# The x transposes of a gated mix of linear attention and a token MLP: from TensorE to DMA, with the first loads in another order

## The chip, the cores and the metric

The kernel runs on one core of a Trainium2 chip. The metric is the device time of one execution in microseconds; the median of three runs of the kernel before is 162.86 us (162.6 to 163.35). Lower is better.

## The reference

The input `x` has 2048 tokens of 512 features, in bfloat16. Two branches work on it and a gate mixes them.

```python
g = sigmoid((x * gate_w).sum(-1, keepdims=True))
# branch A: linear attention, 32 heads of 16
q, k, v = heads(x @ wqkv)
phi = lambda t: where(t > 0, t + 1, exp(t)) + 1e-6
kv = einsum("bhsd,bhse->bhde", phi(k), v);  z = phi(k).sum over s
o = einsum(phi(q), kv) / (einsum(phi(q), z) + 1e-6);  a = o @ wo
# branch B: an MLP over the tokens, after a layer norm over the features
h = layernorm(x);  u = gelu(einsum("bsd,sf->bdf", h, w1) + b1)
b = (einsum("bdf,fs->bds", u, w2) + b2) transposed back
out = g * a + (1 - g) * b
```

`wqkv` is 512 x 1536, `wo` 512 x 512, `w1` 2048 x 1792 and `w2` 1792 x 2048.

## The kernel before, in words

Tokens are cut into 16 tiles of 128 (`NT`), features into four blocks of 128 (`ND`). Two layouts of x are kept on the chip: `xs`, with tokens on the partitions, which is a plain load, and `xT`, with features on the partitions. TensorE multiplies over the partitions, so the projections to q and k need `xT`; the layer norm, the gate and the products below need `xs`.

The scheduler is off (`tc.manual_schedule()`, L123): each engine and each queue runs its instructions in the order of the program, and PSUM is a ring of eight banks, all of one tag. DMAs that SP and ACT issue share eight completion semaphores in turn, so the ninth DMA is issued only when the first has landed, and so on.

The stages of TensorE are, in order:

1. `warm_up`: matmuls on a constant, while the first loads are under way.
2. A head for tiles 0 to 2 (`HEADS = 3`): twelve 128x128 transposes on TensorE against an identity (`transpose_part`, through the helper on L110), whose results DVE (L212) and ACT (L210) copy from PSUM to `xT` (`copy_part`); the k projection of these tiles is put between them in parts (`k_part`), and the layer-norm statistics of tiles 0 and 1 (`ln_step`) follow on DVE.
3. The K loop, tiles 3 to 15: four matmuls of the k projection (`kacc <- wk_sb, xT`), then `k_phi`, which is an exponential on ACT (L216) and two instructions on DVE (L217, L220) that give `pk`; then, four tiles behind (`LAG = 4`), four matmuls that add x^T phi(k) of one tile into four banks that stay held (`g_tile`, `gacc <- pk, xs`); then, five tiles behind, the layer-norm statistics of one tile on DVE (L240, L241).
4. The last four `g_tile`, and then the first third of the MLP's first product (`uacc`) with the q projection (`qacc`) put between, the rest of `uacc`, and per token tile the output of branch A (`aps`) and the second product of the MLP (`yps`).

The head and the K loop hold 64 `kacc` and 64 `gacc` matmuls of 512 columns in all.

The loads go out on two queues. SP issues x tile 0, x tile 1, block 2 of Wk; then, after a small copy on DVE (L156) that writes two columns of `xT` and needs x tile 0, the DMA transposes of tiles 3 to 4 and 5 to 7 straight from memory into `xT` (`load_xT`, L132), then x tiles 3 and 4 to 7, then the transposes of 8 to 11, x 8 to 11, the transposes of 12 to 15, x 12 to 15, Wq, and the MLP's first weights in chunks. ACT issues blocks 0 and 1 of Wk, x tile 2 and block 3 of Wk.

Of the kernel before, what the change touches and what calls it, by code (L numbers as in the profile page):

```python
# [7 lines left out]
ACT = mybir.ActivationFunctionType  # L8
# [7 lines left out]
def kernel(  # L16
# [13 lines left out]
    nc = tc.nc  # L30
    P = nc.NUM_PARTITIONS
# [9 lines left out]
    ND = D // P  # L41
# [24 lines left out]
    def keep(shape, dtype, name):  # L66
        return persist.tile(shape, dtype, name=name, tag=name)

    def bank(name, dtype=FP32):
        return ps.tile([P, SC], dtype, name=name, tag="bank")  # L70

    xs = keep([P, NT, D], BF16, "xs")
    hs = keep([P, NT, D], BF16, "hs")
    xT = keep([P, ND, S], BF16, "xT")
# [15 lines left out]
    ident = keep([P, P], BF16, "ident")  # L90
# [18 lines left out]
    def mm(o, lhsT, rhs, start, stop, **kw):  # L109
        nc.tensor.matmul(o, lhsT=lhsT, rhs=rhs, start=start, stop=stop, **kw)  # L110
# [14 lines left out]
    def load_x(q, t0, n):  # L125
        q.dma_start(out=xs[:, t0 : t0 + n, :], in_=x_view[:, t0 : t0 + n, :])

    def load_wk(q, k, n):
        q.dma_start(out=wk_sb[:, k : k + n, :], in_=wqkv_view[:, k : k + n, D : 2 * D])

    def load_xT(t0, n):
        nc.sync.dma_start(  # L132
            out=xT[:, :, t0 * P : (t0 + n) * P], in_=X[t0 * P : (t0 + n) * P, :], transpose=True
        )

    load_x(nc.sync, 0, 1)
    load_wk(nc.scalar, 0, 2)
    load_x(nc.sync, 1, 1)
    load_x(nc.scalar, 2, 1)
    load_wk(nc.sync, 2, 1)  # L140
    load_wk(nc.scalar, 3, 1)
    nc.vector.memset(ones_f[:], 1.0)
    nc.vector.memset(mhalf[:], -0.5)
    nc.gpsimd.memset(ident[:], 0.0)
# [1 line left out]
        out=ident[:], in_=ident[:], compare_op=ALU.not_equal, fill=1.0, base=0,  # L146
# [5 lines left out]
        out=maskQ[:], in_=maskH[:].rearrange("p (a m) -> p m a", m=2), op=ALU.max, axis=AX.X  # L152
    )
    nc.gpsimd.memset(brow[:], 0.0)

    nc.vector.tensor_copy(  # L156
        out=xT[:, :, 3 * P : 3 * P + 2],
        in_=xs[:, 0, 0 : 2 * ND].rearrange("p (k c) -> p k c", k=ND),
    )
    load_xT(3, 2)  # L160
    load_xT(5, 3)
    load_x(nc.sync, 3, 1)
    load_x(nc.sync, 4, 4)
    for t0, n in ((8, 4), (12, 4)):
        load_xT(t0, n)
        load_x(nc.sync, t0, n)
    nc.sync.dma_start(out=wq_sb[:], in_=wqkv_view[:, :, 0:D])
    w1c = []
    for c, (j0, nb) in enumerate(w1_chunks):
        w = wpool.tile([P, NT, FB * P], BF16, name="w1c", tag="wc")  # L170
        w1c.append(w)
        for t0 in range(0, NT, 8) if c == 0 else (0,):
            t1 = t0 + 8 if c == 0 else NT
            nc.sync.dma_start(
                out=w[:, t0:t1, : nb * P], in_=w1_view[:, t0:t1, j0 * P : (j0 + nb) * P]
# [6 lines left out]
    def load_small():  # L182
        nc.gpsimd.dma_start(out=brow[0:NF, :], in_=B_b1.rearrange("(f q) -> f q", q=P))
        nc.gpsimd.dma_start(out=brow[NF : NF + NT, :], in_=B_b2.rearrange("(f q) -> f q", q=P))
        nc.gpsimd.dma_start(
            out=gw_b[:], in_=gate_w.rearrange("(o d) -> o d", o=1).to_broadcast([P, D])
        )
# [3 lines left out]
    def warm_up(n, cols=SC):  # L191
        for _ in range(n):
            mm(wps[:, :cols], warm[:, 0:P], warm[:, :cols], True, True)

    act_warm = keep([P, 1], FP32, "act_warm")
    nc.scalar.activation(out=act_warm[:], in_=ones_f[:], func=ACT.Exp)
    warm_up(6)

    pts = {}

    def transpose_part(t, k0, k1):
        pt = pts[t, k0, k1] = bank("pt")
        for k in range(k0, k1):
            mm(pt[:, k * P : (k + 1) * P], xs[:, t, k * P : (k + 1) * P], ident[:], True, True)

    def copy_part(t, k0, k1, on_act):
        src = pts.pop((t, k0, k1))[:, k0 * P : k1 * P].rearrange("p (k s) -> p k s", k=k1 - k0)
        dst = xT[:, k0:k1, t * P : (t + 1) * P]
        if on_act:
            nc.scalar.activation(out=dst, in_=src, func=ACT.Copy)  # L210
        else:
            nc.vector.tensor_copy(out=dst, in_=src)  # L212

    def phi(dst, acc):
        e = work.tile([P, SC], BF16, name="e", tag="e", bufs=6)
        nc.scalar.activation(out=e[:], in_=acc[:], func=ACT.Exp)  # L216
        nc.vector.tensor_scalar(  # L217
            out=e[:], in0=e[:], scalar1=1.0, scalar2=PHI_EPS, op0=ALU.min, op1=ALU.add
        )
        nc.vector.scalar_tensor_tensor(  # L220
            out=dst, in0=acc[:], scalar=0.0, in1=e[:], op0=ALU.max, op1=ALU.add
        )
# [3 lines left out]
    def k_part(t, ks):  # L226
        if t not in kaccs:
            kaccs[t] = bank("kacc")
        for k in ks:
            mm(  # L230
                kaccs[t][:], xT[:, k, t * P : (t + 1) * P], wk_sb[:, k, :],
                k == 0, k == ND - 1,
            )

    def k_phi(t):
        phi(pk[:, t, :], kaccs.pop(t))

    def ln_stats(t):
        stats = work.tile([P, nc.vector.BN_STATS_DIM], FP32, name="stats", tag="stats", bufs=2)
        nc.vector.bn_stats(out=stats[:], in_=xs[:, t, :])  # L240
        nc.vector.bn_aggr(out=mv[:, t, :], in_=stats[:])  # L241

    def ln_rstd(g):
        s = slice(g * TPC, (g + 1) * TPC)
        nc.vector.tensor_scalar_add(out=veps[:, s], in0=mv[:, s, 1], scalar1=EPS)
        nc.gpsimd.tensor_tensor(out=rstd[:, s], in0=veps[:, s], in1=mhalf[:], op=ALU.pow)

    def ln_shift(g):
        s = slice(g * TPC, (g + 1) * TPC)
        nc.vector.scalar_tensor_tensor(  # L250
            out=nmr[:, s], in0=mv[:, s, 0], scalar=-1.0, in1=rstd[:, s],
            op0=ALU.mult, op1=ALU.mult,
        )

    def ln_apply(t):
        nc.scalar.activation(  # L256
            out=hs[:, t, :], in_=xs[:, t, :], func=ACT.Identity,
            scale=rstd[:, t : t + 1], bias=nmr[:, t : t + 1],
        )
# [3 lines left out]
    def g_tile(t):  # L263
        if not gacc:
            gacc.extend(bank("gacc") for _ in range(ND))
        for k in range(ND):
            mm(gacc[k][:], xs[:, t, k * P : (k + 1) * P], pk[:, t, :], t == 0, t == NT - 1)
# [15 lines left out]
    def ln_step(u):  # L283
        ln_stats(u)
        if u % TPC == TPC - 1:
            ln_rstd(u // TPC)

    HEADS = 3
    for k0, k1 in ((0, 1), (1, 2), (2, ND)):
        transpose_part(0, k0, k1)  # L290
        copy_part(0, k0, k1, k0 == 2)
    k_part(0, range(2))
    for k0, k1 in ((0, 1), (1, 2), (2, ND)):
        transpose_part(1, k0, k1)
    for k0, k1 in ((0, 2), (2, ND)):
        transpose_part(2, k0, k1)
    copy_part(1, 0, 1, False)
    copy_part(1, 1, 2, True)
    copy_part(2, 0, 2, False)
    copy_part(2, 2, ND, True)  # L300
    copy_part(1, 2, ND, False)
    k_part(1, range(2))
    k_part(2, range(2))
    ln_step(0)
    for t in range(HEADS):
        k_part(t, (2,))
    for t in range(HEADS):
        k_part(t, (3,))
        k_phi(t)
    ln_step(1)  # L310
    LAG = 4
    LN_LAG = 5
    APPLY = 10
    for t in range(HEADS, NT):
        k_part(t, range(ND))
        k_phi(t)
        if t >= LAG:
            g_tile(t - LAG)
        if t > LN_LAG + 1:
            ln_step(t - LN_LAG)  # L320
        if t == TPC - 1 + LN_LAG:
            load_small()
        if t >= APPLY:
            ln_apply(t - APPLY)
        if t in (TPC + LN_LAG, 2 * TPC + LN_LAG):
            ln_shift((t - LN_LAG) // TPC - 1)
# [133 lines left out]
    for j in range(NB0, NF):  # L460
        c, jj = divmod(j, FB)
# [30 lines left out]
        out=gg[:], in0=gth[:], scalar1=0.5, scalar2=0.5, op0=ALU.mult, op1=ALU.add  # L492
    )
    nc.vector.tensor_scalar(
        out=c1[:], in0=gth[:], scalar1=-0.5, scalar2=0.5, op0=ALU.mult, op1=ALU.add
# [3 lines left out]
    for t in range(NT):  # L499
        c, tl = divmod(t, TPC)  # L500
        aps = bank("aps")
        for j in range(ND):
# [3 lines left out]
            out=a_sc[:], in_=aps[:], func=ACT.Identity,  # L506
            scale=gg[:, t : t + 1], bias=c2[:, t : t + 1],
        )
        for c0, W in ((0, 2 * P), (2 * P, P), (3 * P, P)) if t == NT - 1 else ((0, D),):
            cs = slice(c0, c0 + W)  # L510
            yps = bank("yps")
            for f in range(NF):
# [6 lines left out]
                out=ot[:, :W], in0=yps[:, :W], scalar=c1[:, t : t + 1], in1=a_sc[:, cs],  # L519
# [35 lines left out]
```

## Time and profile before

| | |
|---|---|
| median of the runs | 162.86 us (162.6 to 163.35) |
| span of the profiled execution, first to last instruction | 160.8 us |
| median less span | 2.06 us |
| TensorE busy | 156.3 us, 97% of the span |
| DVE busy | 124.8 us, 78% |
| ACT busy | 72.8 us, 45% |
| start of the first MLP matmul, which ends the K stage | 32.49 us |

The profile shows one execution. The record lists no time of its own for it besides the span; the 2.06 us between span and median lie around the program. "PE" is TensorE's matmuls, "PEld" its weight loads, which overlap them. A matmul of 512 columns is listed with 379 ns, but the next one starts some 216 ns after it, since matmuls are pipelined: four take 0.86 us. "SPq" and "ACTq" are the queues on which SP and ACT issue DMAs; the time of such a row is that of issuing, and the landing of the data is listed apart.

### The profile page before, as it was taken

How to read it: one execution, taken by the hardware profiler on the slowest of the kernel's cores; microseconds unless marked ns; L12 is line 12 of the kernel's file. 1: busy time of each engine (PE TensorE's matmuls, PEld its weight loads, DVE VectorE, ACT ScalarE, POOL GpSimd, SP SyncE). 2: the span in 40 equal slices, each digit the busy share in tenths (PEclk: the TensorE clock that was granted, in tenths of full speed). 3: DMA queues.
4: the chain of work that ended last, by engine and by line, in shares of the span. 5: the costliest groups of instructions: out<-in, count | busy, mean ns of one | idle time of the engine just before them, and what ended most of it. 6: DMA issues, size and time to landing. Idle time of an engine off the chain costs nothing.

```text
span 160.8 us, 2241 instructions
## 1 busy us (share of the span) xinstructions
PE 156.3 (97%) x826; PEld 72.6 (45%) x840; DVE 124.8 (78%) x276; ACT 72.8 (45%) x114; POOL 7.3 (5%) x17
## 2 busy tenths in 40 slices
PE   7999999999999999999999999999999999999993
PEld 2444444444444444444444444444444444444462
DVE  1599999769999998756999999676999999711122
ACT  3552476654978483059873330237433442111110
POOL 3000332002020000000000000000000000000000
PEclk9999999999999999999999999999999999999999
DMA  5999999999970007600930689501000001110001
GB/s 165 229 235 238 274 335 295 359 348 348 335 177 0 0 0 236 225 0 5 335 120 2 186 270 288 169 33 37 33 33 33 33 33 60 47 60 33 33 33 33
DMA packets 29369, 22.94 MB, mean 143 GB/s; under 512 B 7824, under 2 KB 29328, under 8 KB 29360
## 3 DMA queue, kind: packets, MB, share of 16 engines
q1 hardware_dynamic: 28400, 21.89, 46.1%
q10 hardware_dynamic: 848, 0.79, 1.4%
q0 software_dynamic: 112, 0.14, 0.7%
q8 instruction: 6, 0.10, 0.3%
q14 instruction: 3, 0.02, 0.0%
HBM read 19.01 MB, written 2.10 MB: 131 GB/s over the span
## 4 chain that ended last, share of the span: by engine, by line
PE 94%; DVE 3%; issue 1%; ACT 0%
PE uacc L110 30%; PE yps L110 30%; PE aps L110 9%; PE qacc L110 8%; PE gacc L110 8%; PE kacc L110 7%; PE wps L110 2%; DVE pk L220 1%; DVE e L217 1%; DVE stats L240 0%; ACT e L216 0%; PE kvps L110 0%; PE pt L110 0%; PE w2ps L110 0%; DVE ot L518 0%
## 5 line engine op out<-in xcount | busy, mean ns | idle before, releaser
L110 PE MATMUL uacc<-hs,w1c 128*128 128x512 bf16 (+1 forms) x230 | 51.2, 379 | 0.3 <-issue 0.2
L110 PE MATMUL yps<-uT,w2c 128*128 128x512 bf16 (+2 forms) x247 | 50.8, 355 | 0.3
L110 PEld LDWEIGHTS <-w2c 128*128 128x128 bf16 x252 | 23.6, 98 | 25.2
L110 PEld LDWEIGHTS <-w1c 128*128 128x128 bf16 (+1 forms) x233 | 21.8, 98 | 26.0 <-issue 0.2
L505 ACT ACTIVATE a_sc<-aps,c,gg 128x512 f32<-128x512 f32 x16 | 12.4, 774 | 31.2 <-PE aps L110 15.5
L518 DVE SCALAR_TENSOR_TENSOR ot<-yps,c,a_sc 128x512 bf16<-128x512 f32 (+2 forms) x18 | 12.3, 688 | 15.4 <-PE yps L110 11.7
L339 ACT ACTIVATE uT<-uacc,bcol 128x512 bf16<-128x512 f32 x14 | 9.3, 686 | 17.5 <-PE uacc L110 17.4
L110 PE MATMUL aps<-W2sb,pqT 128*128 128x512 bf16 x63 | 16.4, 379 | 0.1
L110 PE MATMUL qacc<-xT,wq_sb 128*128 128x512 bf16 x61 | 16.1, 379 | 0.2
L110 PE MATMUL kacc<-wk_sb,xT 128*128 128x512 bf16 x63 | 15.9, 380 | 0.2
L404 DVE STREAM_TRANSPOSE zT<-pz 128x512 f32<-128x512 f32 x16 | 11.3, 705 | 6.0 <-ACT pz L403 6.0
L110 PE MATMUL gacc<-pk,xs 128*128 128x512 bf16 x63 | 15.6, 379 | 0.0
L256 ACT ACTIVATE hs<-xs,nmr,rstd 128x512 bf16<-128x512 bf16 x16 | 12.8, 805 | 2.3 <-DVE nmr L250 2.3
L403 ACT ACTIVATE pz<-pqT,zcol 128x512 f32<-128x512 bf16 x16 | 11.4, 714 | 4.8 <-DVE ot L518 4.7
L216 ACT ACTIVATE e<-kacc 128x512 bf16<-128x512 f32 x16 | 9.2, 596 | 9.7 <-PE kacc L110 9.6
L216 ACT ACTIVATE e<-qacc 128x512 bf16<-128x512 f32 x16 | 9.5, 594 | 7.7 <-PE qacc L110 7.7
L413 DVE STREAM_TRANSPOSE rex<-rd 128x512 bf16<-128x512 bf16 x16 | 11.4, 712 | 0.6
L220 DVE SCALAR_TENSOR_TENSOR pk<-kacc,e 128x512 bf16<-128x512 f32 x16 | 11.1, 692 | 0.6
L220 DVE SCALAR_TENSOR_TENSOR pqT<-qacc,e 128x512 bf16<-128x512 f32 x16 | 11.1, 691 | 0.6
L406 DVE TENSOR_REDUCE den<-zT 128x32 f32<-128x512 f32 x16 | 11.0, 686 | 0.6
L110 PEld LDWEIGHTS <-xs 128*128 128x128 bf16 x76 | 7.2, 100 | 8.3 <-DMA xs<-in_A_x_dram 0.6
L240 DVE BATCH_NORM_STATS2 stats<-xs 128x6 f32<-128x512 bf16 x16 | 10.9, 683 | 0.0
(59 smaller groups left out, 99.3 us busy)
## 6 DMA issues: line engine op xcount, KB each, us to landing
w2c<-in_B_w_dram SPq DMA_DIRECT2D x8, 896.0 KB, 5.8
w1c<-in_B_w_dram SPq DMA_DIRECT2D x2, 2048.0 KB, 15.7
w1c<-in_B_w_dram SPq DMA_DIRECT2D x3, 1024.0 KB, 9.7
out_dram<-ot SPq DMA_DIRECT2D x13, 128.0 KB, 1.7
xs<-in_A_x_dram SPq DMA_DIRECT2D x3, 512.0 KB, 4.5
wq_sb<-in_A_wqkv_dram SPq DMA_DIRECT2D x1, 512.0 KB, 6.6
wv_sb<-in_A_wqkv_dram SPq DMA_DIRECT2D x1, 512.0 KB, 10.4
wo_sb<-in_A_wo_dram SPq DMA_DIRECT2D x1, 512.0 KB, 9.1
```

The costliest lines, as they stand in the source:

```text
L110: nc.tensor.matmul(o, lhsT=lhsT, rhs=rhs, start=start, stop=stop, **kw)
L216: nc.scalar.activation(out=e[:], in_=acc[:], func=ACT.Exp)
L220: nc.vector.scalar_tensor_tensor(out=dst, in0=acc[:], scalar=0.0, in1=e[:], op0=ALU.max, op1=ALU.add)
L240: nc.vector.bn_stats(out=stats[:], in_=xs[:, t, :])
L256: nc.scalar.activation(out=hs[:, t, :], in_=xs[:, t, :], func=ACT.Identity, scale=rstd[:, t : t + 1], bias=nmr[:, t : t + 1],)
L339: nc.scalar.activation(out=uT[:, j, :], in_=acc[:], func=ACT.Gelu_apprx_tanh, bias=bcol[:, j : j + 1])
L403: nc.scalar.activation(out=pz[:], in_=seg, func=ACT.Copy, scale=zcol[:, j : j + 1])
L404: nc.vector.transpose(out=zT[:], in_=pz[:])
L406: nc.vector.tensor_reduce(out=den[:], in_=zT[:].rearrange("p (a d) -> p a d", d=HEAD), op=ALU.add, axis=AX.X)
L413: nc.vector.transpose(out=rex[:].rearrange("p (a d) -> p a d", d=HEAD), in_=rd[:].unsqueeze(2).to_broadcast([P, SC // HEAD, HEAD]),)
L505: nc.scalar.activation(out=a_sc[:], in_=aps[:], func=ACT.Identity, scale=gg[:, t : t + 1], bias=c2[:, t : t + 1],)
L518: nc.vector.scalar_tensor_tensor(out=ot[:, :W], in0=yps[:, :W], scalar=c1[:, t : t + 1], in1=a_sc[:, cs], op0=ALU.mult, op1=ALU.add,)
```

## The change

The TensorE transposes, their copies, the head for tiles 0 to 2 and the small copy that held the first DMA transpose go. All 16 tiles come into `xT` by DMA transposes, and the first is the first DMA that SP issues. ACT issues Wk alone, in two halves. Plain x tiles are put between the later transposes on SP. The warm-up has eight matmuls in place of six. The K loop starts at tile 0, and the statistics of tiles 0 and 1 move into it.

```diff
-    load_x(nc.sync, 0, 1)
+    load_xT(0, 2)
     load_wk(nc.scalar, 0, 2)
-    load_x(nc.sync, 1, 1)
-    load_x(nc.scalar, 2, 1)
-    load_wk(nc.sync, 2, 1)
-    load_wk(nc.scalar, 3, 1)
+    load_wk(nc.scalar, 2, 2)
+    load_xT(2, 2)
+    load_xT(4, 2)
+    load_x(nc.sync, 0, 2)
+    load_xT(6, 2)
+    load_x(nc.sync, 2, 4)
...
-    nc.vector.tensor_copy(
-        out=xT[:, :, 3 * P : 3 * P + 2],
-        in_=xs[:, 0, 0 : 2 * ND].rearrange("p (k c) -> p k c", k=ND),
-    )
-    load_xT(3, 2)
-    load_xT(5, 3)
-    load_x(nc.sync, 3, 1)
-    load_x(nc.sync, 4, 4)
-    for t0, n in ((8, 4), (12, 4)):
+    for t0, n, x0, m in ((8, 3, 6, 4), (11, 3, 10, 3), (14, 2, 13, 3)):
         load_xT(t0, n)
-        load_x(nc.sync, t0, n)
+        load_x(nc.sync, x0, m)
...
-    warm_up(6)
+    warm_up(8)
...
-    HEADS = 3
-    for k0, k1 in ((0, 1), (1, 2), (2, ND)):
-        transpose_part(0, k0, k1)
-        copy_part(0, k0, k1, k0 == 2)
-    k_part(0, range(2))
...
-    for t in range(HEADS):
-        k_part(t, (3,))
-        k_phi(t)
-    ln_step(1)
+    HEADS = 0
     LAG = 4
     LN_LAG = 5
     APPLY = 10
     for t in range(HEADS, NT):
         k_part(t, range(ND))
         k_phi(t)
         if t >= LAG:
             g_tile(t - LAG)
-        if t > LN_LAG + 1:
+        if t >= LN_LAG:
             ln_step(t - LN_LAG)
```

The functions `transpose_part` and `copy_part` are removed with it.

More of the change, by code (lines that the diff above doesn't have):

```diff
@@ L196 @@
     nc.scalar.activation(out=act_warm[:], in_=ones_f[:], func=ACT.Exp)
-    warm_up(6)
[L199 to L212, printed above, removed]
+    warm_up(8)
     def phi(dst, acc):
@@ L286, in ln_step @@
             ln_rstd(u // TPC)
-    HEADS = 3
-    for k0, k1 in ((0, 1), (1, 2), (2, ND)):
-        transpose_part(0, k0, k1)
-        copy_part(0, k0, k1, k0 == 2)
-    k_part(0, range(2))
[L293 to L304, printed above, removed]
-    for t in range(HEADS):
-        k_part(t, (2,))
-    for t in range(HEADS):
-        k_part(t, (3,))
-        k_phi(t)
-    ln_step(1)
+    HEADS = 0
     LAG = 4
```

## The prediction

> **What bounds the kernel now.** I read the page's first and fourth parts, then the chain in order of time, then the DMA queues' issues and their landings, then the DMA share in short stretches. The page:
>
> ```profile
> PE 156.3 (97%) x826; PEld 72.6 (45%) x840; DVE 124.8 (78%) x276; ACT 72.8 (45%) x114; POOL 7.3 (5%) x17
> ```
>
> TensorE is busy 97% of the span, and the page's chain of what ended last is 94% TensorE. So only what keeps it without work counts; removed work on DVE or ACT counts for nothing by itself. The chain in order of time, head and end of the K stage:
>
> ```profile
> 0.84 2.72 PE wps L110 x6
> 3.56 0.12 PE pt L110
> ...
> 4.06 0.62 PE kacc L110 x2
> 4.68 0.46 PE pt L110 x8
> 5.14 1.90 PE kacc L110 x8
> ...
> 28.18 4.32 PE gacc L110 x20
> 32.49 0.65 PE uacc L110 x3
> ```
>
> The warm-up covers the first loads, and from 3.36 us on (the first transpose of x) TensorE works almost without a gap. From 5.14 us it is dense to 32.49, where the K stage ends. That gives the yardstick: the stage has 128 matmuls, four take 0.864 us (20 take 4.32), so 27.65 us, and 32.49 - 27.65 = 4.84. The old head costs as much as if dense K work began at 4.84 us. The change wins or loses by when its own first K matmul starts, plus the stalls after that.
>
> Where the loads stand: a queue row of the timeline (start, us of issuing), then the issues of three short windows, whose last column is us from issue to landing. The first two are the first DMAs of ACT and SP, issued at 0.80 and 0.81 us; the transposes are those issued at 3.45 and 7.79:
>
> ```profile
> 3.45 3.20 SPq L132 DMA_TRANSPOSE xT<-in_A_x_dram  x2
> ```
>
> ```profile
> wk_sb<-in_A_wqkv_dram ACTq DMA_DIRECT2D x1, 256.0 KB, 3.1
> xs<-in_A_x_dram SPq DMA_DIRECT2D x1, 128.0 KB, 2.4
> ...
> xT<-in_A_x_dram SPq DMA_TRANSPOSE x1, 3.8
> ...
> xT<-in_A_x_dram SPq DMA_TRANSPOSE x1, 5.7
> ```
>
> A plain tile needs 2.4 us to land, a transposed pair 3.8. The stretches of the DMA engines (columns: stretch; PE, PEld, DVE, ACT, POOL busy; clock; DMA share; GB/s):
>
> ```profile
> 2.10:5.20 3.10, 3.03 (x19) 1.53 (x18) 1.21 (x6) 2.17 (x5) 0.09 (x1) 1.00 0.91 304
> 5.20:6.70 1.50, 1.50 (x8) 0.62 (x9) 1.40 (x4) 0.36 (x1) 0.00 (x0) 1.00 1.12 182
> ...
> 8.30:9.40 1.10, 1.10 (x7) 0.48 (x5) 1.06 (x3) 1.01 (x3) 0.00 (x0) 1.00 0.66 152
> 9.40:10.60 1.20, 1.20 (x8) 0.55 (x6) 1.17 (x4) 0.42 (x1) 0.00 (x0) 1.00 1.05 349
> 10.60:13.10 2.50, 2.45 (x12) 1.11 (x12) 2.40 (x6) 1.02 (x2) 0.00 (x0) 1.00 1.30 235
> 13.10:13.90 0.80, 0.80 (x5) 0.39 (x4) 0.77 (x3) 0.17 (x1) 0.00 (x0) 1.00 0.65 192
> ```
>
> Plain loads alone run at 304 to 349 GB/s. A lone transposed pair (5.20 to 6.70) keeps the engines full, share 1.12, at 182 GB/s. The stretches at 8.30 and 13.10 are the changeovers from a transpose to a plain load on the same queue: share 0.65, half the rate or less.
>
> **What goes.** Twelve transposes (1.2 us busy) and the first `kacc` between them fill 3.36 to 5.14; that is already in the yardstick. Five copies on DVE (3 x 0.29 + 2 x 0.42 = 1.7 us), three on ACT (1.05 us) and the 0.17 us copy L156 stood ahead of the first phi, where both engines now would idle anyway: 0. ACT issues one DMA fewer (0.49 us) ahead of its table load: 0, its first exponential comes after 5 us. POOL's queue is not moved. SP no longer waits for x tile 0 (2.1 us) before its first transpose.
>
> **The first K matmul.** It needs the pair of tiles 0 and 1, and Wk. Lower end: the pair takes the 3.8 us of the row at 3.45, and Wk beside it costs nothing: 0.81 + 3.8 = 4.61. Upper end: Wk is served in full before the pair is done. Wk is 512 KB = 0.524 MB, at 349 to 370 GB/s (peaks in the head) 1.42 to 1.5 us: 4.61 + 1.42 = 6.03. At 3.45 us Wk was nearly through (its last block, issued at 1.82, landed 4.2 later, at 6.0), so the 3.8 us is close to a price without company. I take 5.7, near the upper end, because the share of 1.12 says that a lone pair leaves the engines no room; I take 0.33 off since the same engines pass transposes at 235 GB/s when the queue is full (10.60 to 13.10) against 182, 0.3 us on 262 KB. If Wk wins the engines, the pair is last; if the pair wins, the second half of Wk is last, and only its third matmul (0.43 us on) needs it: much the same start. So 5.7 - 4.84 = +0.86 us.
>
> [...]
>
> **The warm-up.** Weight loads of the warm-up are 0.43 us apart, so eight end at 0.84 + 8 x 0.43 = 4.3 us: hidden under the wait for the pair, 0. It leaves TensorE idle from 4.3 to 5.7, a gap that the old trace does not have. From 5.14 on matmuls are 0.216 us apart, half of 0.43, so the head ran at a slower rate that ended by 4.06. Ends: 0, or the slow rate again for as long as in the old head, six matmuls x 0.214 = 1.3 us. I take 0: the rate held after 4.06 though 0.4 us of copies and small transposes stood between, and 1.3 stays for the range. [...]
>
> **The stream behind it.** Step times from the first K matmul (0): pairs 2-3 and 4-5 are needed at 1.73 and 3.46; x tile 0 at 4.33 (after five K tiles), pair 6-7 at 6.92, x 2 at 7.79, transposes 8-10 at 10.38, x 6 at 14.7, transposes 11-13 at 15.6, 14-15 at 20.8. The two transposes at 3.45 start 1.38 us apart, so SP issues a pair in about that time, and its queue stays filled from 0.81 on. Served in order: a transposed tile takes 0.64 us (four in the 2.5 of 10.60 to 13.10), a plain one 0.36 (128 KB at 349 to 370 GB/s), a changeover loses 0.6 (1.1 x (1 - 152/349); the one at 13.10 lost 0.4). With the data of pair 0-1 through at 5.3 and 0.4 for landing: pair 2-3 lands at 7.0 (needed 7.4), 4-5 at 8.3 (9.2), x 0-1 at 9.6 (10.0), 6-7 at 10.9 (12.6), x 2-5 at 12.9 (13.5), 8-10 at 14.8 (16.1), x 6-9 at 16.8 (20.4), 11-13 at 18.8 (21.3), 14-15 at 21.7 (26.5). Nothing is late, but x 0-1 and x 2-5 are early by only 0.4 and 0.6 us. A DMA waits for the landing of the eighth before it (transposes 8-10 for pair 0-1): all landed by then, 0. Stalls: between 0 and, if a changeover loses its whole 1.1 us twice and a pair keeps the lone 1.5 us (0.12 a tile more, on six tiles), 1.0 + 0.75 - 0.6 = 1.1; I take 0.15, near the lower end, since the fuller queue is the nearer row. Wq then lands near 25 (needed 33) and the first MLP weights near 28 (needed 33.4): hidden.
>
> **DVE.** Two statistics steps (0.69 + 0.18 = 0.82 us in pace each) move from the head into loop steps 5 and 6. Each step then is 1.80 us on DVE against 1.73 on TensorE. Before, `pk` of tile 15 ended at 30.40 and its `gacc` began at 31.63, a margin of 1.2. Counting phi from 1.6 us after the first K matmul, the new `pk` 15 ends 25.9 after it, needed at 26.8: margin 0.9, cost 0; up to 0.4 if x 0-1 is late, since the statistics stand ahead of phi on DVE.
>
> **Sum.** 0.86 + 0.15 = 1.0 us. The profiled span would go from 160.8 to 161.8, and with the same 2.06 us around it the median from 162.86 to 163.9.
>
> **The rivals.**
> - *The pair lands like the one at 3.45* (on the other side: not slower): Wk and the transposes interleave without cost, start 4.6 to 5.2, no stalls. For it: shares up to 1.30 where both kinds of transfer are in flight; against it: 182 GB/s at full share. It decides from a start below 5.6 us. 162.6 to 163.3, at its middle 162.9 us.
> - *The plain tiles come late in the loop*: the margins of 0.4 and 0.6 are gone, TensorE waits on `xs` in two places and DVE's statistics with it: +1.0 more, 164.9. For it: the changeovers; against it: the queue is never empty, and in the old trace no `gacc` waited for x.
> - *The slow rate returns or lasts in the gap*: +1.3 more, 165.2. For it: the gap is new; against it: it is shorter than the busy stretch before it.
> - *A gain*: only if the pair lands by 4.0, faster than any transpose here.
>
> **How the numbers follow.** The forecast has 0.45 (own range 163.4 to 164.4), the first rival 0.27, late tiles 0.15, the slow rate 0.10, a gain 0.03. A 0.5% change, 0.8 us, is about what a measurement here tells from none. Slower (above 163.7) is two thirds of the forecast and both late cases, with a little of the first rival's edge: 0.58; faster 0.04; same 0.38. The range from 162.7 to 165.2 leaves out a quarter of the first rival (0.07), half of the slow rate (0.05), the gain and the two late cases together (0.05).
>
> **What would show it.** First `kacc` at 5.7 us with its weight load released by the DMA of `xT` (or of `wk_sb`); none of the `pt` rows but that of the biases; TensorE's idle time in the slice from 4.3; the first `uacc` at 33.5; no waits on `xs` in the loop. I am wrong if the first `kacc` starts below 5.2 or above 6.2, if its first matmuls are 0.43 us apart, or if weight loads wait for `xs` by more than 0.5 us in sum.

## The result: the K stage ends 3.2 us later

The changed kernel takes 165.28 us (median of ten runs, 163.53 to 166.96) against 163.07 us for the kernel before (ten runs, 162.6 to 163.54). The ratio is 1.0097, with a 95% interval of 1.0068 to 1.0126: slower by about 1.6 us. The ratio goes by the means and leaves out the run of 166.96 us, which the record lists as slow, so it is smaller than the 2.2 us between the medians. The runs of the changed kernel fall into two groups, four from 163.5 to 163.8 us and six from 165.1 up: about 0.5 and 2.4 us above the kernel before. One of the upper group was profiled: 165.67 us, span 163.9 us.

The page of the changed kernel still has TensorE busy for nearly all of the span, but a DMA now stands in the chain:

```profile
PE 158.5 (97%) x830; PEld 72.4 (44%) x830; DVE 123.3 (75%) x270; ACT 72.1 (44%) x111; POOL 7.3 (4%) x17
...
PE 95%; DMA 3%; DVE 0%; issue 0%
```

The chain of the changed kernel in order of time (start, us, what):

```profile
0.81 5.35 DMA xT<-in_A_x_dram
...
6.21 6.13 PE kacc L110 x20
12.34 0.86 PE gacc L110 x4
...
31.33 4.32 PE gacc L110 x20
35.65 0.65 PE uacc L110 x3
```

The first transposed pair takes 5.35 us to land and the first K matmul starts at 6.21 us. The K stage ends at 35.65 us where it ended at 32.49 before, 3.16 us later; the span is 3.1 us longer. After the K stage nothing changed: 163.9 - 35.65 = 128.25 us against 160.8 - 32.49 = 128.31.

The delay has two parts. Twenty K matmuls at full rate take 20 x 0.216 = 4.32 us, but here they take 6.13. The weight loads of the changed kernel (start, us; one load goes ahead of each matmul, 830 of each on the page) show where:

```profile
6.20 0.13 PEld L110 LDWEIGHTS <-xT 128*128 128x128 bf16 x2 [2.69 <-DMA xT<-in_A_x_dram]
6.61 0.15 PEld L110 LDWEIGHTS <-xT 128*128 128x128 bf16 x1 [0.27 <-issue]
7.04 0.15 PEld L110 LDWEIGHTS <-xT 128*128 128x128 bf16 x1 [0.28 <-issue]
7.46 0.15 PEld L110 LDWEIGHTS <-xT 128*128 128x128 bf16 x1 [0.28 <-issue]
7.89 0.15 PEld L110 LDWEIGHTS <-xT 128*128 128x128 bf16 x1 [0.27 <-issue]
8.32 0.15 PEld L110 LDWEIGHTS <-xT 128*128 128x128 bf16 x1 [0.28 <-issue]
8.74 0.15 PEld L110 LDWEIGHTS <-xT 128*128 128x128 bf16 x1 [0.28 <-issue]
9.17 0.15 PEld L110 LDWEIGHTS <-xT 128*128 128x128 bf16 x1 [0.27 <-issue]
9.59 0.96 PEld L110 LDWEIGHTS <-xT 128*128 128x128 bf16 x5 [0.27 <-issue]
```

Up to 9.59 us they are 0.43 us apart, then 0.216 (five in 0.96 us). Eight intervals at the slow rate cost 8 x 0.214 = 1.71 us. So the start is late by 6.21 - 4.84 = 1.37 us and the slow matmuls add 1.71: together 3.08 of the 3.16. The rest of the K stage is dense, so nothing is left for late x tiles. The column of the granted clock reads 1.00 in these stretches: the slow rate is to be seen only in the spacing of the instructions.

Why TensorE is without work, in the timeline (start, us of work):

```profile
0.81 4.83 SPq L132 DMA_TRANSPOSE xT<-in_A_x_dram  x3
0.81 0.14 PEld L110 LDWEIGHTS <-const-bfloat16-1.0 128*128 128x128 bf16 x2 [0.81 <-issue]
0.84 3.57 PE L110 MATMUL wps<-const-bfloat16-1.0 128*128 128x512 bf16 x8 [0.84 <-PEq L496]
```

The warm-up ends at 4.41 us and TensorE idles for 1.8 us. The DMA engines meanwhile (stretch; PE, PEld, DVE, ACT, POOL busy; clock; DMA share; GB/s):

```profile
2.10:4.90 2.80, 2.32 (x6) 0.59 (x4) 0.13 (x1) 1.18 (x2) 0.09 (x1) 1.00 1.09 290
4.90:5.70 0.80, 0.00 (x0) 0.00 (x0) 0.00 (x0) 0.00 (x0) 0.00 (x0) 1.00 1.33 111
5.70:7.00 1.30, 0.79 (x2) 0.28 (x3) 0.00 (x0) 0.00 (x0) 0.00 (x0) 1.00 1.27 286
```

They are full up to 4.9 us (share 1.09, 290 GB/s from 2.1 us), and where Wk's packets run out (17 of its 544 come after 4.9 us) all that moves is 111 GB/s, at a share of 1.33, for 0.8 us.

### The profile page after: what moved, and what is told of

Its sections match the earlier page's. It is cut to its first block, busy times and chain, and to the rows that moved or that the text cites. A ratio compares the mean times of both kernels' runs of the same rounds, so it can differ in the third digit from the quotient of the medians.

```text
span 163.9 us, 2223 instructions
## 1 busy us (share of the span) xinstructions
PE 158.5 (97%) x830; PEld 72.4 (44%) x830; DVE 123.3 (75%) x270; ACT 72.1 (44%) x111; POOL 7.3 (4%) x17
## 4 chain that ended last, share of the span: by engine, by line
PE 95%; DMA 3%; DVE 0%; issue 0%
PE uacc L110 30%; PE yps L110 30%; PE kacc L110 10%; PE qacc L110 8%; PE gacc L110 8%; PE aps L110 8%; DMA xT<-in_A_x_dram 3%; PE kvps L110 0%; PE w2ps L110 0%; DVE ot L475 0%; PE pt L302 0%
## 5 line engine op out<-in xcount | busy, mean ns | idle before, releaser
L110 PE MATMUL kacc<-wk_sb,xT 128*128 128x512 bf16 x64 | 17.4, 410 | 1.8 <-DMA xT<-in_A_x_dram 1.8
L196 DVE TENSOR_SCALAR e<-e 128x512 bf16<-128x512 bf16 x32 | 9.0, 281 | 9.0 <-ACT e L195 9.0
L110 PEld LDWEIGHTS <-xT 128*128 128x128 bf16 x64 | 6.6, 104 | 11.3 <-DMA xT<-in_A_x_dram 2.7
```

The lines of the kernel that those rows point to most:

```text
L196: nc.vector.tensor_scalar(out=e[:], in0=e[:], scalar1=1.0, scalar2=PHI_EPS, op0=ALU.min, op1=ALU.add)
```

## The experiments

Two causes were to be told apart and priced. **Company:** the pair is late because Wk shares the DMA engines with it; the rival is that the first transposing DMA is slow by itself. **Gap:** the idle 1.8 us keeps TensorE at the slow rate; the rival is that the rate is released at a time of its own, whatever TensorE does. The runs with the gap filled, with little company, with the pair split (thirteen warm-ups) and with a gap in the kernel before were made together on one chip, with the kernel before at 162.99 us (162.56 to 164.05).

**The gap filled.** The changed kernel with

```diff
-    warm_up(8)
+    warm_up(13)
```

> The changed kernel with 13 warm-up matmuls in place of 8, so that TensorE has work until the first pair of transposed tiles lands at about 6.2 us. Theory (the idle gap from 4.4 to 6.2 us keeps the slow rate): the first K matmul stays at 6.2 to 6.4 us, but the first K matmuls are 0.216 us apart and not 0.43; the 1.7 us of the eight slow ones go, the span is 162.0 to 162.4 and the median 163.5 to 164.0. Rival (the rate is released at a time of its own, whatever TensorE does): still up to eight K matmuls at 0.43, the median stays at 165 or more. Second rival (nothing but the later start counts): median within 0.3 us of the changed kernel.

164.15 us (163.61 to 164.47, six runs); the ratio to the kernel before is 1.0070, 1.0047 to 1.0093. No run is in the upper group. The chain of this kernel:

```profile
0.85 5.54 PE wps L110 x13
6.39 4.32 PE kacc L110 x20
10.71 0.86 PE gacc L110 x4
```

All thirteen warm-ups ran at the slow rate (5.54 us), the first K matmul came at 6.39, later than without them, and yet the twenty K matmuls take 4.32 us: none is slow. The K stage ends at 34.02 us. The median was a little above the range expected; the slow warm-ups, not the pair, now set the start. So five more matmuls, which compute nothing, take 1.6 us off the profiled span (163.9 to 162.3). That is against a run of the upper group: the lower group, 163.5 to 163.8 us, stays a little faster than the filled kernel, and over all runs the ratio falls only from 1.0097 to 1.0070, with intervals that overlap.

**Little company.** The same, with one block of Wk loaded and read by all four matmuls of a projection (three quarters of Wk left out):

```diff
-    load_wk(nc.scalar, 0, 2)
-    load_wk(nc.scalar, 2, 2)
+    load_wk(nc.scalar, 0, 1)
...
-                kaccs[t][:], xT[:, k, t * P : (t + 1) * P], wk_sb[:, k, :],
+                kaccs[t][:], xT[:, k, t * P : (t + 1) * P], wk_sb[:, 0, :],
```

> The changed kernel with 13 warm-up matmuls, and only one of the four blocks of Wk (128 KB) loaded; all four matmuls of a k projection read that block, so three quarters of Wk are left out of the result. It prices the company of Wk on the first pair. Theory (Wk and the pair share the DMA engines): the pair, which landed 5.35 us after its issue, lands 4.0 to 4.6 us after it, and the first K matmul starts at 4.9 to 5.5 us. Rival (the first transposing DMA of the program is slow by itself): it still lands 5.2 us or more after its issue.

The DMA issues of this kernel's first microseconds (last column: us from issue to landing):

```profile
wk_sb<-in_A_wqkv_dram ACTq DMA_DIRECT2D x1, 128.0 KB, 2.3
xT<-in_A_x_dram SPq DMA_TRANSPOSE x1, 4.1
```

Those of the kernel with all of Wk and thirteen warm-ups, for the same window:

```profile
wk_sb<-in_A_wqkv_dram ACTq DMA_DIRECT2D x1, 256.0 KB, 2.9
xT<-in_A_x_dram SPq DMA_TRANSPOSE x1, 5.3
```

The pair lands 1.2 us sooner for 384 KB less of Wk, that is 0.39 MB at 330 GB/s. With all of Wk it took 5.3 to 5.5 us in three profiles (the changed kernel, this one with thirteen warm-ups and the one without a warm-up, below). So company is a cause, and the first transposing DMA does not need 5.2 us by itself. The pair alone was not measured: the 3.8 us in the kernel before are not without company either, since 0.45 MB of plain loads, blocks 2 and 3 of Wk among them, moved there from 3.45 to 4.9 us. The first K matmul started at 5.83 us and not at 4.9 to 5.5 as expected, because the thirteen warm-ups held it (4.99 us in the chain of this kernel). One run: 163.55 us.

**The pair split.** Thirteen warm-ups, with

```diff
-    load_xT(0, 2)
-    load_wk(nc.scalar, 0, 2)
+    load_xT(0, 1)
+    load_wk(nc.scalar, 0, 1)
+    load_xT(1, 1)
+    load_wk(nc.scalar, 1, 1)
     load_wk(nc.scalar, 2, 2)
```

> The changed kernel with 13 warm-up matmuls; the first pair is issued as two transposes of one tile each, and Wk as blocks 0, 1 and then 2 to 3. The first K matmul needs tile 0 and block 0 only, 256 KB in place of 512. Theory (what counts is how many bytes must be through): the first K matmul starts 0.5 to 1.0 us earlier, at 5.2 to 5.7 us, unless the 13 warm-ups at the slow rate hold it until 6.4; median 0.3 to 1.0 us below that of the 13 warm-ups alone. Rival (a fixed time of about 5 us from the first issue to the first landing when plain and transposing loads mix): start at 6.0 or later, median within 0.3 us of it.

164.53 us (163.84 to 164.75; ratio 1.0090, 1.0066 to 1.0113). Tile 0 landed 3.8 us after its issue, at 4.6, but the warm-ups, all slow, held the first K matmul until 6.42 us, as the chain has it:

```profile
0.84 5.57 PE wps L110 x13
6.42 4.32 PE kacc L110 x20
```

The case that the expectation named came about, and the run says nothing on what an early tile 0 is worth. So it was run again with nine.

**The pair split, nine warm-ups.**

> As the split pair (tile 0 alone first, Wk as blocks 0, 1 and 2 to 3), with 9 warm-up matmuls, which end by 4.7 us at the slow rate, in place of 13, which held the first K matmul until 6.42 although tile 0 had landed 3.8 us after its issue. Theory (what must be through decides the start): first K matmul at 4.7 to 5.3 us, later ones paced by blocks 1 to 3 and tile 1, the span 161.0 to 162.5, the median 0.5 to 1.3 us below that of the split with 13. Rival (the first landing gains nothing since the rest of Wk or the next tile is late by as much): waits on wk_sb or xT of 1 us and more in the first K tiles, median as with 13 within 0.3 us.

163.97 us (163.71 to 164.25) with the kernel before at 163.17 us in that set of runs, on the same chip; ratio 1.0049, 1.0037 to 1.0062. The weight loads of this kernel from its first K matmul on:

```profile
4.33 0.10 PEld L110 LDWEIGHTS <-xT 128*128 128x128 bf16 x1 [0.39 <-DMA xT<-in_A_x_dram]
4.64 0.15 PEld L110 LDWEIGHTS <-xT 128*128 128x128 bf16 x1 [0.21 <-issue]
5.07 0.15 PEld L110 LDWEIGHTS <-xT 128*128 128x128 bf16 x1 [0.28 <-issue]
5.72 0.10 PEld L110 LDWEIGHTS <-xT 128*128 128x128 bf16 x1 [0.51 <-issue]
6.29 0.55 PEld L110 LDWEIGHTS <-xT 128*128 128x128 bf16 x4 [0.46 <-DMA xT<-in_A_x_dram]
7.81 0.11 PEld L110 LDWEIGHTS <-xT 128*128 128x128 bf16 x2 [0.98 <-DMA xT<-in_A_x_dram]
```

The first K matmul starts 1.6 us sooner (4.64 us, and 6.25 with thirteen, both by the timeline). The load at 5.72 comes 0.65 us after the one before it. The profile names no releaser, but blocks 2 to 3 of Wk, issued at 1.70, landed 4.0 us later, at 5.7, and the third K matmul, which reads block 2, starts at 5.72. Then TensorE waits for tile 1 at 6.3 and for pair 2 to 3 at 7.8. The K stage ends at 33.89 us, 0.15 us before that of the split with thirteen. In the medians, each over the kernel before of its own set of runs, it is +0.80 against +1.54 us: a gain of 0.7, of which the slow warm-ups' hold is part. The truth lies between the two theories: the start moved as the first says, the waits came as the second says.

**A gap in the kernel before.**

```diff
-    warm_up(6)
+    warm_up(2)
```

> The kernel before with two warm-up matmuls in place of six, so that TensorE idles from about 1.7 us to the first transpose at 3.4 us. Theory (work in the first microseconds is what releases the full rate): the head runs slowly for longer, matmuls at 0.43 us apart until some 3 us after the dense work begins, 0.8 to 2.0 us slower than before. Rival (the rate is released at a time of its own): no change within 0.3 us.

163.71 us (163.57 to 165.01; ratio 1.0072, 1.0040 to 1.0103). The chain of this kernel's head:

```profile
3.93 1.01 PE kacc L110 x2
4.94 0.85 PE pt L110 x8
5.79 4.50 PE kacc L110 x18
```

The eight transposes take 0.85 us, 0.46 before; the K stage ends at 33.60 us, 1.1 later than before, though the first x tile and the first half of Wk landed about as they did (2.2 and 3.1 us after issue, 2.4 and 3.1 before). Here work taken from the first three microseconds was paid back at the slow rate. In the medians it is +0.72 us, just below what the theory expected, but four of the seven runs lie from 163.57 to 163.71 us and three from 164.49 to 165.01. The ratio over all of them makes it 1.2 us; the profiled run, 163.66 us, is of the lower four. These may be two groups again, but seven runs do not show it.

**No warm-up at all** (the changed kernel without the call):

> The changed kernel without any warm-up. Theory (work releases the full rate, some 3 to 6 us after it begins): the first K matmul starts at 6.2 us and matmuls stay 0.43 us apart for about 3 us or more, so 7 to 14 slow ones and +1.5 to +3.0 us in every run against the 13 warm-ups: median 165.5 to 167.2 with no run below 165. Rival (the rate is released at a time of its own): some runs near 163.6, as among those of the changed kernel.

166.16 us (165.71 to 166.99, five runs; ratio 1.0189, 1.0166 to 1.0212): no run in the lower group. The chain:

```profile
6.37 7.29 PE kacc L110 x20
...
32.66 4.32 PE gacc L110 x20
36.97 0.65 PE uacc L110 x3
```

7.29 - 4.32 = 2.97 us is fourteen slow matmuls. Start, dense stage and slow matmuls add up: 6.37 + 27.65 + 14 x 0.214 = 37.0, measured 36.97. A release at a time of its own would have left some runs near 163.6. Here none of five is below 165.7, and the rate changes only at about 12.2 us, later than in any other kernel; that rival falls.

**A mix of both kernels**, to see whether either part is worth keeping: x tile 0 plain and first on SP, transposed on TensorE as before; then DMA transposes from tile 1 on; Wk alone on ACT; six warm-ups.

```diff
-    load_xT(0, 2)
+    load_x(nc.sync, 0, 1)
     load_wk(nc.scalar, 0, 2)
+    load_xT(1, 1)
     load_wk(nc.scalar, 2, 2)
     load_xT(2, 2)
     load_xT(4, 2)
-    load_x(nc.sync, 0, 2)
+    load_x(nc.sync, 1, 1)
...
-    HEADS = 0
+    HEADS = 2
+    for k0, k1 in ((0, 1), (1, 2), (2, ND)):
+        transpose_part(0, k0, k1)
+        copy_part(0, k0, k1, k0 == 2)
+    for t in range(HEADS):
+        k_part(t, range(2))
+    for t in range(HEADS):
+        k_part(t, range(2, ND))
+        k_phi(t)
```

> A mix: x tile 0 is a plain load, first on SP, and transposed on TensorE as before (four transposes); SP then issues DMA transposes of tile 1, 2 to 3, 4 to 5, x tile 1, and the rest as changed; ACT loads Wk alone; six warm-ups; K of tiles 0 and 1 is done blocks 0 to 1 first, then 2 to 3. Theory (the first microseconds are bound by bytes, 768 KB by the time K of tile 1 ends): TensorE is fed from 3.3 us, waits some 0.5 to 1 us for tile 1 or for the second half of Wk, the K stage ends as if dense from 4.6 to 5.3 us, median 162.7 to 163.6. Rival (transposes in company stall both kinds of load): tile 1 lands after 6 us, median 164 or more.

163.61 us (163.03 to 165.69, twelve runs), the kernel before at 163.17; ratio 1.0061, 1.0026 to 1.0096. Seven runs lie from 163.0 to 163.7 and five from 165.1 to 165.7. In the profiled one, of the lower group, tile 1 lands at 5.81 us, 4.55 after its issue, and TensorE's weight loads wait 1.42 us for it:

```profile
5.85 3.57 PEld L110 LDWEIGHTS <-xT 128*128 128x128 bf16 x18 [1.42 <-DMA xT<-in_A_x_dram]
```

The K stage ends at 33.22, as if dense from 5.6, later than the 4.6 to 5.3 expected and sooner than the rival's tile 1 after 6 us. It does not beat the kernel before.

**The gap of the mix filled.**

```diff
-    for t in range(HEADS):
-        k_part(t, range(2))
+    k_part(0, range(2))
+    warm_up(4)
+    k_part(1, range(2))
```

> The mix with four more warm-up matmuls put where its TensorE waited for tile 1 (1.4 us, from 4.4 to 5.85 us), after the first two K matmuls. Its 12 runs fell into two groups, seven from 163.0 to 163.7 and five from 165.1 to 165.7. Theory (an idle gap in the first microseconds lets the slow rate stay): the upper group goes, the K stage still ends near 33.2 us, median 163.1 to 163.6. Rival (the upper group is something else, in the loads for example): it stays at about four runs in ten.

163.95 us (163.41 to 164.20, six runs on another chip, with the kernel before at 162.96; ratio 1.0058, 1.0041 to 1.0075). The upper group is gone a second time, but over all runs nothing is gained: the ratio was 1.0061 without the fillers. The median is higher than expected: in the profiled run the four fillers end at 6.29 us, and only then does K of tile 1 start, which started at 5.85 without them; the stage ends at 33.49.

```profile
5.09 1.21 PE wps L110 x4
6.29 3.88 PE kacc L110 x18
```

With six runs, none in the upper group could be luck at four in ten (0.6^6 = 5%); together with the same finding on the changed kernel, where six in ten were (0.4^6 = 0.4%), that is unlikely.

**Eight warm-ups in the kernel before.**

> The kernel before with eight warm-up matmuls in place of six: this part of the change alone. There the first x tile lands at about 3.2 us and nothing hides the two more. Theory (in the changed kernel they are free since the pair lands later): here they hold the first transposes until 4.0 to 4.3 us, +0.4 to +0.9 us, median 163.5 to 164.0. Rival (they release the full rate earlier and pay for themselves): within 0.3 us of before.

163.47 us (162.91 to 164.05), the kernel before at 162.96 on that chip; ratio 1.0043, 1.0026 to 1.0060: 0.5 us. In its chain the warm-ups end at 4.02 us, 3.56 in the kernel before, and the first transposes wait for them. What the changed kernel has for nothing costs 0.5 us where the data is there.

Of all kernels, the span less the end of the K stage is 128.2 to 128.7 us. The differences arise in the first ten microseconds, and without a warm-up in the first thirteen.

## Why the prediction was right, and where it was not

The direction held; the mechanism was half right. By the ratio the time is 162.86 x 1.0097 = 164.4 us, inside the range; the median of ten, 165.28, lies just above its end of 165.2. That it came so near is in part luck: +1.6 us is the mean of a group at +0.5 and one at +2.4, and neither is the +1.0 of the sum. Two of the three signs of being wrong came about: a first `kacc` above 6.2 us (6.21) and first matmuls 0.43 us apart.

- **The yardstick** (128 matmuls, 27.65 us, dense from 4.84) held: the start, the slow matmuls and this sum give the end of the K stage to 0.1 us in the changed kernel and in that without warm-up.
- **The first K matmul**, taken at 5.7 us, came at 6.21. The failed term is the 0.33 us taken off for transposes that pass faster when the queue is full. The runs showed Wk's price in full: 1.2 us for 384 KB, and the landing at 6.16 is just above the upper end, 6.03. That Wk was nearly through at 3.45 us in the kernel before was a misreading: blocks 2 and 3 were still to come, so the 3.8 us are no price without company. Instead of passing faster, the transposes passed at no more than 111 GB/s for 0.8 us where Wk's packets ran out. While Wk's packets lasted, both queues moved: in the changed kernel 125 packets on Wk's queue and 150 on that of the transposes from 4.1 to 4.6 us. The pair landed at 6.16 us, just behind the second half of Wk (issued at 1.27, landed 4.7 us later, at about 6.0).
- **The warm-up's gap**, taken at 0, is the step that failed most. It was listed as a rival of +1.3 us with a chance of 0.10, but six runs of ten are in the upper group, and in the one that was profiled it costs 1.71 us. The reason given for the 0 was a rate that "held after 4.06"; that row shows a rate already released, and in the changed kernel all eight warm-ups, which end at 4.4 us, when the gap begins, are at the slow rate. The runs show when the spacing changed, and that the time moved: with work from 0.84 us on, it had changed by 4.06 us in the kernel before, at about 5.0 with thirteen warm-ups and little company, and only at about 6.2 with thirteen warm-ups and all of Wk, that is after 3.2 to 5.4 us. Why it moves is not shown.
- **Stalls in the stream** (0.15 taken, up to 1.1 feared): none. From 9.6 to 35.65 us TensorE is dense, and no weight load waits for a DMA, so the rival of late plain tiles is wrong here. x tiles 0 and 1 landed at 8.8 us (issued at 5.68, 3.1 us to land) where 9.6 was worked out, and the late start gave all later tiles more room.
- **DVE**: `pk` of tile 15 ends at 33.57 us and its `gacc` begins at 34.79, a margin of 1.2 us where 0.9 was worked out; no cost, as forecast. The removed copies and transposes bought nothing, as forecast.
- **The sum**, +1.0 us, set against about +1.6 by the ratio, +3.1 in the profiled span. The 2.06 us taken to lie around the span mixed a median with one profile: the changed kernel's profiled run is 165.67 - 163.9 = 1.77 us above its span, and a run of the kernel before with a span of 160.8 us took 162.56.
- **The rival on the other side** (the pair lands as in the row at 3.45) is ruled out by 5.3 us with Wk against 4.1 with a quarter of it.

The lower group of the changed kernel, 163.53 to 163.75 us, was not profiled. That in these runs the rate was released before the gap or during it is an inference from the filled and the unwarmed kernels, and not shown. Their spans fit it: 161.8 to 162.0 us, less 128.3 after the K stage and 27.65 of dense matmuls, leave by estimate 5.9 to 6.1 us for the start, with no room for slow matmuls. Whether the upper group keeps the slow rate through the gap, or is released and falls back, is not shown either.

## What to carry to other kernels

In the first microseconds of this kernel the first matmul was set by all bytes in flight on the DMA engines before its operand was through, and not by that operand's size alone: the transposed pair, first on its queue, landed after 5.3 us with all of Wk on the other queue and after 4.1 with a quarter of it. Look at the gap between the warm-up and the first real matmul: here it could bring the slow rate into the real work (1.71 us in the profiled run), and that showed as two groups of runs. Filling it made the runs even, but of the mean it gained about 0.4 us (changed kernel, with intervals that overlap) or nothing (the mix). A warm-up that outlasted the data cost time here: thirteen held the first K matmul of the split pair until 6.42 us, with tile 0 landed at 4.6, and eight in place of six cost the kernel before 0.5 us. In the split pair it was better to start real matmuls at the slow rate (+0.80 us over the kernel before) than to fill the time (+1.54).

## What was not expected of the hardware

The same kernel ran in two groups about 1.9 us apart (163.6 and 165.5 us), and the mix showed the same (163.3 and 165.4), on one core with nothing else changed; filling the gap removed the upper group both times. The granted clock of the profile stayed at 1.00 over stretches where matmuls of 512 columns were 0.43 us apart in place of 0.216. And where the packets of a plain load on one queue ran out, a transposing DMA on the other moved at most 111 GB/s for 0.8 us at full DMA share, where it came to 286 after that. The kernel before has such a stretch too (93 GB/s from 5.5 to 6.0 us at a share of 1.03); what holds it up is not shown.
